# Retention and mixture of experts: the first expert's first 16 products in two halves, and the work around them in another order

## The chip, the cores and the metric

The kernel runs on one core of a Trainium2 chip. A core has five engines with queues of their own: TensorE (PE in the profile; its weight loads are PEld), VectorE (DVE), ScalarE (ACT), GpSimd (POOL) and SyncE (SP), which mostly issues transfers; the transfers themselves run on the core's 16 DMA engines. The metric is the device time of one execution in microseconds, the median of three runs.

## The reference

Retention (a linear attention with decay) over 4 x 8 heads, 768 positions in blocks, and then a layer of 8 experts over its output, where each row goes to the one expert that a gate chooses:

```python
x = attn_out.transpose(0, 2, 1, 3).reshape(B * S, H * D)      # 3072 x 512
logits = x @ w_gate
e_idx = np.argmax(logits, axis=1)
for e in range(E):                                            # 8 experts
    mask = e_idx == e
    h = np.maximum(x[mask] @ w1[e], 0.0)                      # 512 -> 1024
    ye = h @ w2[e]                                            # 1024 -> 512
    out[mask] = gate_w[mask, None] * eom[mask, e, None] * ye
```

`gate_w` is the softmax weight of the chosen expert, `eom` a sigmoid gate.

## The kernel before, in words

**Two stages.** The first computes x in 24 tiles of 128 rows (n = 0 to 23; `NTILE` is 24, `LAST` is 20): transposes, score products, products with v and with the running state. For each group of tiles it works out the gate's logits, the choice of an expert (`route_choose`) and the place of each row in its expert's list (`route_place`), and GpSimd scatters a record of each row into a table in DRAM (`tab_d`, `place_scatter`). The rows themselves are transposed (`stage_d2`, tile `xn`) and stored to `x_d` in DRAM by SP. The second stage takes the experts in order of their number of rows. For each, GpSimd gathers its rows from `x_d` (`gather`, tile `xg`, 32 rows to a transfer), VectorE transposes them (`x_turn`, tile `y`), TensorE multiplies by w1 (`up`, banks `ph`), ScalarE and VectorE take the ReLU apart into two parts (`hhi`, `hlo`), and TensorE multiplies by w2 (banks `py` and `pyr`). Weights come in 32 loads of 1 MB, nearly all by SP (`load_piece`, tile `raw`, three buffers; the second piece is issued by GpSimd) and are split into two parts on ScalarE and VectorE (`whi`, `wlo`).

**The first expert bridges the two.** Which expert has most rows is decided after the first 16 tiles (`RES`). Its first 256 rows are gathered from these, in eight transfers, while the last tiles are still computed: gathers 0 to 3 feed the first transpose `x_turn(0, 0)`, gathers 4 to 7 the second, `x_turn(0, 1)`; both write the same tile `y`. Its other rows, up to 192, are found among tiles 16 to 23 once these have been counted (`mark`, `found`), and gathered as transfers 8 to 13 from `x_d`, after all of x has been stored. So the first expert is worked in two halves: h = 0 (256 columns) and h = 1 (192 columns).

**What sets the order.** It is written out by hand. The list `units` holds the products of half 0 (32 of `up_mm`, each one matmul of 256 columns in fp32, which the trace shows as two instructions; then 16 steps of three products for the w2 side of rows 0 to 255). `fill(k)` issues the next k of them on TensorE, and `settle` the evictions that they have made ready. Between the fills stands the tail of the first stage, on all engines' queues: the places of tiles 20 and 21 (`place`), the choice and places of tiles 22 and 23 (`last`), the marks, two stores of x (`stage_d2(n - 3, 2)` for tiles 20 and 21, called store A here, and `stage_d2(n - 1, 2)` for 22 and 23, store B), two weight loads (`load_piece(2)`, `load_piece(3)`) and the counts. Each engine takes its own instructions strictly in that order. At the end stand the late gathers (`gather(0, 8)`), the sorting of the other experts, the loads of index and tables (which read `tab_d` and so wait for its scatters), and more weight loads.

Of the kernel before, what the change touches and what calls it, by code (L numbers as in the profile page):

```python
# [23 lines left out]
def kernel(  # L24
# [17 lines left out]
    P = 128  # L42
    NPAIR = H // 2
# [6 lines left out]
    NKC = DM // P  # L50
# [884 lines left out]

    hts = {}

    def up_mm(p, fc, h, kc):
        sl = slice((fc % 4) * P, (fc % 4 + 1) * P)
        r = cols(p, h)  # L940
        if kc == 0:
            phs[(p, fc)] = bank(f"ph_{p}_{fc}_{h}")
        if p == 0:
            nb = min(8, NB[p] - 8 * h)
            nc.tensor.matmul(  # L945
                phs[(p, fc)][:, r].rearrange("p (b r) -> p b r", b=nb),
                raws[fc // 4][:, kc, sl],
                ys[(p, h)][:, 0 : nb * P].rearrange("p (b g r) -> p g b r", b=nb, g=NPAIR)[:, kc],
                start=(kc == 0),
                stop=(kc == NKC - 1),  # L950
            )
            return
        whi, wlo = wparts[(p, 0, fc // 4)]
        xhi, xlo = xts[(p, kc)]
        mm3(
            phs[(p, fc)][:, r], (whi[:, kc, sl], wlo[:, kc, sl]), (xhi[:, r], xlo[:, r]),
            kc == 0, kc == NKC - 1,
        )
# [6 lines left out]
    def up_act(p, fc, h):  # L965
        if (p, fc) not in hts:
            hts[(p, fc)] = (slot(f"hhi_{p}_{fc}", F32R), slot(f"hlo_{p}_{fc}", F32R))
        hi, lo = hts[(p, fc)]
        ph = phs.pop((p, fc))
        r = cols(p, h)  # L970
        nc.scalar.activation(out=hi[:, r], in_=ph[:, r], func=AF.Relu)  # L971
        parts = [(r, lo[:, r])]
        if p == 0 and h == 1 and SIDE > 0:
            r0, r1 = slice(r.start, SIDE), slice(SIDE, CAP[0])
            parts = [(r0, lo[:, r0]), (r1, hi[:, CAP[0] : 2 * CAP[0] - SIDE])]
        for r, to in parts:
            nc.vector.scalar_tensor_tensor(  # L977
                out=to, in0=ph[:, r], scalar=0.0, in1=hi[:, r].bitcast(F32),
                op0=ALU.max, op1=ALU.subtract,
            )  # L980
# [192 lines left out]
    held = []  # L1173
    units = []
    acts = []
    for fc in range(NFC):
        for kc in range(NKC):
            act = (lambda fc=fc: up_act(0, fc, 0)) if kc == NKC - 1 else None
            units.append((lambda fc=fc, kc=kc: up_mm(0, fc, 0, kc), act))
    for j in range(2):  # L1180
        for fc in range(NFC):
            act = (lambda j=j: emit_rows(0, j, phs.pop((0, "y", j)))) if fc == NFC - 1 else None
# [13 lines left out]
    with tc.manual_schedule():  # L1196
# [124 lines left out]
        place[0]()  # L1321
        x_turn(0, 0)
        logits(LAST + 2, 2)
        x_turn(0, 1)
        stage_d2(n - 3, 2)
        load_piece(2)
        fill(3)
        for f in place[1:]:
            f()
        place_scatter(len(pending))  # L1330
        logit_rows(LAST + 2)
        fill(6)
        at_once(route_choose(LAST + 2, NTILE))
        for b in range(2):
            mark(LAST, b, 1, late_width)
        last = route_place(LAST + 2, NTILE)
        counts = rank_counts("pcount")
        last[0]()
        fill(6)
        stage_d2(n - 1, 2)  # L1340
        load_piece(3)
        for i in (2, 4, 6):
            last[i]()
        for b in range(2):
            mark(LAST + 2, b, 1, late_width)
        pfound = bank("pfound_late")
        for n in range(RES, NTILE):
            found(pfound, n, (n - RES) // B + 1, late_width, n == RES, n == NTILE - 1)
        settle(2)
        for i in (1, 3, 5, *range(7, len(last))):  # L1350
            last[i]()
        place_scatter(len(pending))
        fill(5)
        row_turn(2, pfound, late_width)
        row_index(0, 2)
        row_join(2, late_width)
        gather(0, 8)
        settle()
# [264 lines left out]
```

## Time and profile before

| | us |
|---|---|
| Median of 3 runs | 412.31 (411.94 to 412.67) |
| The profiled execution | 413.83 |
| its span on the core | 412.2 |
| TensorE busy in it | 397.1 (96%) |
| VectorE, GpSimd, ScalarE busy | 280.3, 233.0, 184.0 |
| DMA, mean rate | 192 GB/s |

Times in the views count from the start of the span. A busy share is an average over the whole kernel, and TensorE's 96% says little about one stage; the stage of this change lies between 114 and 147 us. A group of instructions of the timeline gives the start of the first, the time from there to the end of the last, and how many; ends of matmuls are modelled, so that one matmul's duration is longer than the distance to the next, and steps are read from start to start.

### The profile page before, as it was taken

The numbers are of one execution on the slowest core, as the hardware profiler recorded it, in microseconds if no ns is written. First come the engines' busy times: TensorE is split into PE (matmuls) and PEld (weight loads), VectorE is DVE, ScalarE is ACT, GpSimd is POOL, SyncE is SP. The second block draws the span as 40 slices with busy tenths as digits, with TensorE's granted clock in tenths as the row PEclk, the third lists the DMA queues.
The fourth block names the chain that finished last, engine by engine and source line by source line (L and its number), as shares of the span: only waits on it lengthen the run. The fifth ranks groups of instructions, "written<-read, shape, count | busy, mean of one in ns | idle before, by whom it ended". The sixth has DMA issues, their size and how long they took to land.

```text
span 412.2 us, 10314 instructions
## 1 busy us (share of the span) xinstructions
PE 397.1 (96%) x3767; PEld 364.2 (88%) x3767; DVE 280.3 (68%) x798; ACT 184.0 (45%) x450; POOL 233.0 (57%) x305
## 2 busy tenths in 40 slices
PE   8999989799969999999999999999999999999995
PEld 5879978688858898999999999999999989989985
DVE  3858786678867639778669757957965874863611
ACT  3757656578413325446045325604713542542500
POOL 2567877755876777874583666376386266211002
PEclk9999999999989999999999999999999999999998
DMA  9999999998968844744369648757946985461001
GB/s 179 225 206 254 230 220 233 254 224 198 286 196 249 242 164 105 241 147 139 127 185 308 220 130 237 242 183 188 320 151 172 300 258 167 129 214 64 0 26 48
DMA packets 102116, 78.96 MB, mean 192 GB/s; under 512 B 66348, under 2 KB 78128, under 8 KB 102064
## 3 DMA queue, kind: packets, MB, share of 16 engines
q1 hardware_dynamic: 93264, 63.85, 55.5%
q0 software_dynamic: 6544, 14.15, 11.1%
q10 hardware_dynamic: 2256, 0.30, 0.5%
q8 instruction: 30, 0.49, 0.5%
q14 instruction: 22, 0.18, 0.2%
HBM read 62.45 MB, written 16.21 MB: 191 GB/s over the span
## 4 chain that ended last, share of the span: by engine, by line
PE 75%; DMA 12%; SPq 6%; DVE 3%; issue 1%; POOL 1%; ACTq 0%; POOLq 0%; DVEq 0%
PE ph_None L83 10%; PE ph_None L82 10%; PE ph_None L81 10%; PE py L82 6%; PE py L83 6%; PE py L81 6%; PE pyr L82 4%; PE pyr L81 4%; PE pyr L83 4%; SPq L175 3%; PE ps L389 3%; PE ph L945 3%; SPq L168 3%; DMA tab_d<-rec,idx 3%; PE po L433 2%; DMA xg<-x_d,rows 2%
## 5 line engine op out<-in xcount | busy, mean ns | idle before, releaser
L894 POOL DMA_INDIRECT xg<-x_d,rows x103 | 114.5, 1112 | 63.7 <-issue 34.7
L971 ACT ACTIVATE hhi<-ph_None 128x400 fp32r<-128x400 f32 (+4 forms) x56 | 28.1, 501 | 120.5 <-PE ph_None L83 115.6
L136 DVE TENSOR_TENSOR wlo<-raw,whi 128x512 fp32r<-128x512 f32 x120 | 79.6, 684 | 0.7 <-ACT whi L127 0.5
L83 PE MATMUL ph_None<-xhi,wlo 128*128 128x400 f32 (+4 forms) x224 | 76.3, 341 | 0.0
L81 PE MATMUL ph_None<-xhi,whi 128*128 128x400 f32 (+4 forms) x224 | 76.3, 341 | 0.0
L82 PE MATMUL ph_None<-xlo,whi 128*128 128x400 f32 (+4 forms) x224 | 76.3, 341 | 0.0
L127 ACT CAST whi<-raw 128x512 fp32r<-128x512 f32 x120 | 70.0, 614 | 0.0
L977 DVE SCALAR_TENSOR_TENSOR hlo<-ph_None,hhi 128x400 fp32r<-128x400 f32 (+4 forms) x56 | 31.8, 568 | 37.2 <-ACT hhi L971 37.0
L398 DVE TENSOR_TENSOR at<-ps,decay 128x512 f32<-128x512 f32 x48 | 31.2, 683 | 22.5 <-PE ps L389 22.2
L83 PE MATMUL py<-hhi,wlo 128*128 128x400 f32 (+2 forms) x128 | 44.6, 348 | 0.0
L82 PE MATMUL py<-hlo,whi 128*128 128x400 f32 (+2 forms) x128 | 44.6, 348 | 0.0
L81 PE MATMUL py<-hhi,whi 128*128 128x400 f32 (+2 forms) x128 | 44.6, 348 | 0.0
L81 PEld LDWEIGHTS ph_None<-xhi,whi 128*128 128x128 f32 x224 | 42.1, 188 | 0.4
L82 PEld LDWEIGHTS ph_None<-xlo,whi 128*128 128x128 f32 x224 | 42.1, 188 | 0.4
L83 PEld LDWEIGHTS ph_None<-xhi,wlo 128*128 128x128 f32 x224 | 42.1, 188 | 0.3
L1092 POOL DMA_INDIRECT out_dram<-yn,table x12 | 13.3, 1112 | 49.5 <-DVE yn L1165 31.9
L349 ACT COPY qT<-pq 64x256 f32<-64x256 f32 x88 | 34.7, 394 | 2.5 <-PE pq L341 1.7
L81 PE MATMUL pyr<-whi,hhi 128*128 128x512 f32 (+1 forms) x88 | 34.6, 393 | 0.0
L82 PE MATMUL pyr<-wlo,hhi 128*128 128x512 f32 (+1 forms) x88 | 34.3, 390 | 0.0
L83 PE MATMUL pyr<-whi,hlo 128*128 128x512 f32 (+1 forms) x88 | 34.3, 390 | 0.0
L699 POOL DMA_INDIRECT tab_d<-rec,idx x24 | 24.6, 1024 | 14.9 <-DVE rows L853 4.5
L945 PE MATMUL ph<-y,raw 128*128 128x256 f32 (+1 forms) x128 | 26.9, 369 | 3.4 <-issue 3.2
(211 smaller groups left out, 717.2 us busy)
## 6 DMA issues: line engine op xcount, KB each, us to landing
raw<-in_moe_w_dram SPq DMA_DIRECT2D x31, 1024.0 KB
x_d<-xn SPq DMA_DIRECT2D x12, 512.0 KB
qkv<-in_k_dram SPq DMA_DIRECT2D x38, 128.0 KB
qkv<-in_v_dram SPq DMA_DIRECT2D x19, 256.0 KB
qkv<-in_q_dram SPq DMA_DIRECT2D x36, 128.0 KB
yd<-yo SPq DMA_DIRECT2D x12, 256.0 KB
yr<-yd SPq DMA_DIRECT2D x48, 64.0 KB
xg<-x_d,rows POOLq DMA_INDIRECT x103, 3.4
```

The costliest lines, as they stand in the source:

```text
L81: nc.tensor.matmul(ps, a[0], b[0], start=first, stop=False)
L82: nc.tensor.matmul(ps, a[0], b[1], start=False, stop=False)
L83: nc.tensor.matmul(ps, a[1], b[0], start=False, stop=last)
L127: nc.scalar.copy(out=hi, in_=src)
L136: eng.tensor_tensor(out=lo, in0=src, in1=hi.bitcast(F32), op=ALU.subtract)
L349: copies = [lambda r=r, view=view, src=src: nc.scalar.copy(out=view(qT[r]), in_=src) for r, view, src in query_parts(pq)]
L398: nc.vector.tensor_tensor(out=at, in0=ps.rearrange("p (g t) -> p g t", g=NPAIR), in1=dec[:, j], op=ALU.mult)
L699: nc.gpsimd.indirect_dma_start(out=tab_d, out_offset=bass.IndirectOffsetOnAxis(ap=idx, axis=0), in_=rec, in_offset=None, bounds_check=P * ...
L894: nc.gpsimd.indirect_dma_start(out=xg[(p, b // 4)][:, (b % 4) * P : (b % 4 + 1) * P], out_offset=None, in_=x_q[0 : 4 * rows], in_offset=ba ...
L945: nc.tensor.matmul(phs[(p, fc)][:, r].rearrange("p (b r) -> p b r", b=nb), raws[fc // 4][:, kc, sl], ys[(p, h)][:, 0 : nb * P].rearrange(" ...
L971: nc.scalar.activation(out=hi[:, r], in_=ph[:, r], func=AF.Relu)
L977: nc.vector.scalar_tensor_tensor(out=to, in0=ph[:, r], scalar=0.0, in1=hi[:, r].bitcast(F32), op0=ALU.max, op1=ALU.subtract,)
```

## The change

`up_mm` takes a `part`. For fc 0 to 3 of the first expert the product of 256 columns becomes two of 128: part 0 reads the first 512 columns of `y` (rows of gathers 0 to 3), part 1 the second 512. The list `units` has part 0 of fc 0 to 3 first, then part 1 of them, then fc 4 to 7 as before; the eviction comes after part 1. In the tail, the fills and the steps between them are put in another order.

```diff
-    def up_mm(p, fc, h, kc):
+    def up_mm(p, fc, h, kc, part=None):
...
-        if kc == 0:
+        if kc == 0 and not part:
             phs[(p, fc)] = bank(f"ph_{p}_{fc}_{h}")
         if p == 0:
-            nb = min(8, NB[p] - 8 * h)
+            nb, y0 = min(8, NB[p] - 8 * h), 0
+            if part is not None:
+                nb, y0, r = 4, 4 * P * part, slice(P * part, P * part + P)
...
-                ys[(p, h)][:, 0 : nb * P].rearrange("p (b g r) -> p g b r", b=nb, g=NPAIR)[:, kc],
+                ys[(p, h)][:, y0 : y0 + nb * P].rearrange("p (b g r) -> p g b r", b=nb, g=NPAIR)[:, kc],
...
-    for fc in range(NFC):
-        for kc in range(NKC):
-            act = (lambda fc=fc: up_act(0, fc, 0)) if kc == NKC - 1 else None
-            units.append((lambda fc=fc, kc=kc: up_mm(0, fc, 0, kc), act))
+    for part, fcs in ((0, range(4)), (1, range(4)), (None, range(4, NFC))):
+        for fc in fcs:
+            for kc in range(NKC):
+                act = (lambda fc=fc: up_act(0, fc, 0)) if kc == NKC - 1 and part != 0 else None
+                units.append((lambda fc=fc, kc=kc, part=part: up_mm(0, fc, 0, kc, part), act))
...
         logits(LAST + 2, 2)
+        fill(8)
+        for f in place[1:]:
+            f()
+        for b in range(2):
+            mark(LAST, b, 1, late_width)
+        place_scatter(len(pending))
         x_turn(0, 1)
+        logit_rows(LAST + 2)
+        fill(8)
+        at_once(route_choose(LAST + 2, NTILE))
         stage_d2(n - 3, 2)
         load_piece(2)
-        fill(3)
-        for f in place[1:]:
-            f()
-        place_scatter(len(pending))
-        logit_rows(LAST + 2)
-        fill(6)
-        at_once(route_choose(LAST + 2, NTILE))
-        for b in range(2):
-            mark(LAST, b, 1, late_width)
         last = route_place(LAST + 2, NTILE)
+        fill(4)
         counts = rank_counts("pcount")
         last[0]()
-        fill(6)
+        fill(4)
         stage_d2(n - 1, 2)
         load_piece(3)
         for i in (2, 4, 6):
             last[i]()
         for b in range(2):
             mark(LAST + 2, b, 1, late_width)
+        fill(10)
         pfound = bank("pfound_late")
...
-        settle(2)
         for i in (1, 3, 5, *range(7, len(last))):
             last[i]()
         place_scatter(len(pending))
-        fill(5)
+        settle(1)
+        row_index(0, 2)
+        fill(2)
         row_turn(2, pfound, late_width)
-        row_index(0, 2)
         row_join(2, late_width)
```

On TensorE, right behind the logits of the last two tiles (`pl`; `ph_k` is the bank of fc = k, four matmuls each over kc; `raw` the weights):

```order
-L945 MATMUL ph_0_0_2625<-y_0_2605,raw_2390 128x256 x3
+L947 MATMUL ph_0_0_2618<-y_0_2605,raw_2390 128x128 x4
+L947 MATMUL ph_1_0_2623<-y_0_2605,raw_2390 128x128 x4
 L492 MATMUL pl_2607<-ident,lT_2616 128x128
-L945 MATMUL ph_0_0_2625<-y_0_2605,raw_2390 128x256
-L945 MATMUL ph_1_0_2651<-y_0_2605,raw_2390 128x256 x4
-L945 MATMUL ph_2_0_2656<-y_0_2605,raw_2390 128x256
+L947 MATMUL ph_2_0_2653<-y_0_2605,raw_2390 128x128 x4
+L947 MATMUL ph_3_0_2658<-y_0_2605,raw_2390 128x128 x4
+L947 MATMUL ph_0_0_2618<-y_0_2605,raw_2390 128x128 x4
 L741 LDWEIGHTS ones
```

Sixteen half products of part 0 now stand where before nine whole ones stood, and part 1 of fc 0 comes next; the counts (L741) stay behind them.

On VectorE, from the first transpose of gathered rows (`y` from `xg_0`) on; `xn` from `xT` are the transposes for store A, `pr` the places of tiles 20 and 21:

```order
 L911 STREAM_TRANSPOSE y_0_2605<-xg_0_2153 128x512
-L911 STREAM_TRANSPOSE y_0_2605<-xg_1_2373 128x512
-L516 STREAM_TRANSPOSE xn_2619<-xT_2379 128x512
-L516 STREAM_TRANSPOSE xn_2619<-xT_2468 128x512
 L672 TENSOR_REDUCE pr_2601<-ex_2585 128x2
 L663 TENSOR_TENSOR pr_2601<-pr_2601,ebase 128x16
```

The second transpose and the two for store A leave their place ahead of the places of tiles 20 and 21.

Further on in the same queue of the changed kernel, at the end of the choice for tiles 22 and 23 (`cm`, `oh`) and the places of these (`pr`, `sl`):

```order
+L582 TENSOR_REDUCE cm_2664<-pl_2607 128x2
+L583 TENSOR_TENSOR oh_2638<-pl_2607,cm_2664 128x16
+L516 STREAM_TRANSPOSE xn_2677<-xT_2379 128x512
+L516 STREAM_TRANSPOSE xn_2677<-xT_2468 128x512
+L516 STREAM_TRANSPOSE xn_2703<-xT_2519 128x512
+L516 STREAM_TRANSPOSE xn_2703<-xT_2565 128x512
+L663 TENSOR_TENSOR pr_2695<-pr_2695,ebase 128x16
```

All four transposes for stores A and B now stand in a row behind that choice; before, two marks and store B's two stood there. The second transpose of gathered rows stands ahead of the choice, behind the marks of tiles 20 and 21. The order of the instructions on SP and on GpSimd is the same before and after.

## Rows read from the trace of the kernel before

**Rows 1.** Waits of TensorE from 118.2 us on: total, times, longest (us).

```profile
PE ph L945 <- issue: 3.2, 1, 3.2
PE ph L945 <- DVE y L911: 0.2, 1, 0.2
```

**Rows 2.** Stretches: length, busy PE, PEld, DVE, ACT, POOL; PEclk, DMA share, GB/s.

```profile
114.95:118.17 3.22, 0.00 (x0) 0.03 (x1) 0.81 (x2) 0.27 (x1) 2.33 (x3) 1.00 0.19 44
...
119.50:123.00 3.50, 3.50 (x10) 2.80 (x9) 3.29 (x20) 0.69 (x3) 2.73 (x5) 0.51 1.14 374
...
147.00:200.00 53.00, 53.00 (x276) 49.62 (x275) 38.95 (x114) 24.28 (x57) 36.57 (x40) 1.00 0.52 160
```

**Rows 3.** Chain of waits, in order of time: start, length (us), what.

```profile
114.76 2.58 DMA xg<-x_d,rows
...
123.45 5.64 DMA x_d<-xn
129.09 4.27 DMA tab_d<-rec,idx
...
138.44 7.63 DMA xg<-x_d,rows
...
146.69 3.33 PE ph L945 x19
...
157.33 0.23 PE pyr L81
```

**Rows 4.** VectorE's timeline: start, us, instruction, count, idle before and its releaser.

```profile
114.10 0.71 DVE L911 STREAM_TRANSPOSE y<-xg 128x512 f32<-128x512 f32 x1
117.36 0.71 DVE L911 STREAM_TRANSPOSE y<-xg 128x512 f32<-128x512 f32 x1 [2.55 <-DMA xg<-x_d,rows]
118.00 1.26 DVE L516 STREAM_TRANSPOSE xn<-xT 128x512 f32<-128x512 f32 x2
...
120.47 0.21 DVE L496 TENSOR_REDUCE lg<-pl 128x32 f32<-128x64 f32 x1
...
121.65 0.72 DVE L595 TENSOR_SCALAR marks<-slot_no,lead,sl 128x192 bf16<-128x192 bf16 x2
...
136.57 2.50 DVE L136 TENSOR_TENSOR wlo<-raw,whi 128x512 fp32r<-128x512 f32 x4
```

**Rows 5.** Timeline of SP's queue, 119 to 141 us: transfers as issued.

```profile
119.29 0.37 SPq L523 DMA_DIRECT2D x_d<-xn  x1
...
123.45 0.36 SPq L523 DMA_DIRECT2D x_d<-xn  x1
124.01 0.38 SPq L114 DMA_DIRECT2D raw<-in_moe_w_dram  x1
133.37 0.36 SPq L824 DMA_DIRECT2D index<-tab_d  x1
...
134.54 4.22 SPq L114 DMA_DIRECT2D raw<-in_moe_w_dram  x2
```

**Rows 6.** Timeline of POOL: the first and the last of the six late gathers.

```profile
131.37 1.07 POOL L894 DMA_INDIRECT xg<-x_d,rows  x1 [1.29 <-DVE keys L745]
...
138.44 1.50 POOL L894 DMA_INDIRECT xg<-x_d,rows  x1 [0.30 <-issue]
```

**Rows 7.** Stretches as in rows 2, for the DMA share.

```profile
118.60:121.20 2.60, 2.60 (x11) 2.14 (x10) 2.43 (x17) 0.22 (x1) 2.25 (x3) 0.68 0.99 388
121.20:131.20 10.00, 10.00 (x59) 8.64 (x58) 7.08 (x33) 2.35 (x7) 6.72 (x10) 0.91 1.05 289
132.60:134.80 2.20, 2.20 (x12) 1.92 (x12) 2.16 (x5) 1.36 (x3) 1.75 (x2) 1.00 0.25 48
135.50:144.00 8.50, 8.50 (x39) 7.01 (x38) 5.28 (x13) 2.45 (x5) 6.29 (x6) 1.00 0.97 279
```

**Rows 8.** TensorE's timeline: four transposes of 128 columns, 34 products of 256.

```profile
100.03 0.66 PE L341 MATMUL pk<-ident,k 128*128 128x128 f32 x4
...
128.08 7.53 PE L945 MATMUL ph<-y,raw 128*128 128x256 f32 x34
```

**Rows 9.** Weight loads by form, 85 to 150 us: count, busy, mean ns, idle before.

```profile
L945 PEld LDWEIGHTS ph<-y,raw 128*128 128x128 f32 x85 | 16.4, 205 | 6.0 <-issue 3.5 <-PE pyr L83 0.5
```

## The prediction

> **What bounds the kernel now.** I read four views, in this order. First TensorE's own waits: from 118.2 us to the end there are two, 3.2 us at the first product of the first expert and 0.2 us in front of its second half [rows 1]. Then the stretches: TensorE does nothing from 114.95 to 118.17, runs for the 3.5 us from 119.50 to 123.00 at a mean granted share of 0.51 (the 1.2 GHz level), and from 147 on is busy without a gap (53.00 of 53.00 us) [rows 2]. So whatever moves the start of the second half (the 192 late rows, first product at 146.69) moves the end of the kernel by the same amount, and what only moves work before 146.69 is worth nothing by itself.
>
> Third, the chain of waits, to see who sets 146.69 [rows 3]. It is not TensorE's own work. It runs through the second store of x, issued at 123.45, then through gathers, the last of which is issued at 138.44 and lands 7.63 us later, and the transpose y at 146.10. TensorE comes to that point only 0.2 us earlier [rows 1]. So two chains end there together: TensorE's (gap, half clock, products) and the transfers'. The change shortens the first. The question is what it does to the second.
>
> Fourth, the queues under that chain. SP issues store A (tiles 20, 21) at 119.29, a 1 MB weight load right behind it, store B (tiles 22, 23) at 123.45 and another load right behind that [rows 5]. The DMA share is 0.99 from 118.60 to 121.20 and 1.05 from 121.20 to 131.20 [rows 7]: the engines are full, and what SP issues is served in the order of issue. The first late gather goes at 131.37 [rows 6], since it must read what store B wrote (5.64 us to its release in the chain [rows 3]). Then the share falls to 0.25 (132.60 to 134.80) and is 0.97 again from 135.50 to 144.00 [rows 7], when the next loads, issued in a row from 134.54 on [rows 5], run in front of the last gathers: the same kind of gather that took 2.58 us at 114.76 takes 7.63 us at 138.44 [rows 3].
>
> **The change part by part.** *Halves.* The first 16 products (two instructions each, 128x256) become 32 of 128 columns. An instruction of 256 columns costs 0.216 us at full clock: 34 of them in 7.53 us, of which some 0.4 is the modelled tail of the last one, so 33 steps in 7.13 [rows 8]. One of 128 columns with fresh 128x128 weights: four transposes in 0.66 us, less a tail of some 0.29, so 0.123 a step [rows 8], against 0.108 by columns alone. 64 instructions so cost 6.9 to 7.9 us where 32 cost 6.9. Upper bound, if the weight load (205 ns mean [rows 9]) hid under nothing: 64 x 0.205 = 13.1, +6.2 us. I take 0.123, the row nearest in shape: +1.0 us, on TensorE's chain only.
>
> The Trainium skill speaks against halving: "TensorE: Matmul & The Clock Gate", section "Back-to-back issue gap", says that in a stream of weight loads and matmuls both set the spacing, and gives 81 ns for 128 columns in bf16 where columns alone would need about 54. By that ratio an instruction here would cost 0.162 us and the halves +3.5, an estimate from the page; TensorE would then stand 2.5 us later than I put it below, and the third rival would gain on my forecast. The transposes' 0.123 speaks for the smaller price; no product of this shape stands in the trace.
>
> *The gap.* Part 0 needs only the first transpose y, started at 114.10 and 0.71 us long [rows 4], so products start at 114.95 instead of 118.17: 3.2 us. Without the gap nothing puts the clock down at 119.5; rows at the lower level put that at (1 - 0.51) x 3.50 = 1.7 us [rows 2]. TensorE's chain to the second half gets 3.2 + 1.7 - 1.0 = 3.9 us shorter. That is 146.5 - 3.9 = 142.6. It also meets its weights: the second load behind the stores has landed when the share is down, at 132.6 [rows 7]; then come a first quarter on ScalarE (0.6, like VectorE's), four quarters on VectorE in 2.50 us [rows 4], and nine steps of three products at 0.23 us [rows 3] after the last of them: 132.6 + 0.6 + 2.5 + 6.2 = 141.9, plus what the load itself slips (below). From either side TensorE is at the second half at about 142.6.
>
> *VectorE's order.* The second y waits until 117.36 for its gathers, as before; its follower starts at 118.00 [rows 4]. Before, the two transposes for store A came first, then places, choice and marks, then store B's two. Now places and marks fill the wait before 117.36, and behind the second y come the choice (120.47 to 121.65, 1.18 us [rows 4]) and then four transposes. Store A was issued 1.29 us after its first transpose had started at 118.00 [rows 4, 5]; now that starts at 118.00 + 1.18, so A goes at 120.47, **1.18 us later**. Store B goes two more transposes (1.26 us [rows 4]) after A, near 121.7, **1.8 us earlier**. SP's order is the same: A, load, B, load.
>
> *What the transfers do with that.* B is behind A and a 1 MB load in a full queue, so an earlier issue buys nothing, while A's later issue moves the whole queue. Not all 1.18 us: before, A also stood behind the load that POOL had issued, which filled the engines up to 121.2 (share 0.99 [rows 7]), 1.9 us after A's issue. If a store needs as long as that to start in any case, the slip is 1.18; if it starts as soon as the load of 134.54, of which the share shows traffic from 135.5 on (1.0 us), 120.47 + 1.0 = 121.5 against 121.2, so 0.3. Bounds 0.3 to 1.2; I take 0.8, since A has a full queue ahead of it in the trace and the lone load is the farther row. B's landing, the first gather, the scatters behind the second load, SP's index load at 133.37 (which waits for the last scatter, 4.27 us after 129.09 [rows 3]) and the loads behind it all move by it. Gathers and loads keep their order, so the last gather still lands behind a load: **second half at 146.69 + 0.8 = 147.5**.
>
> *POOL* has the same order; its scatters go at its own pace (the last at 129.09 [rows 3]) and are covered by the wait for B. The counts, the places of the last tiles and the join of the late indices are short steps like those of the choice and are hidden by that same wait; uncovered they would cost 1.18 us for every six of them [rows 4].
>
> *The new gap.* TensorE now waits from 142.6 to 147.5, some 4.9 us, against 0.2 before. The one idle stretch of the trace that long, 3.22 us, was followed by 1.2 GHz for about 3.5 us, costing 1.7 [rows 2]. After this one every product lies on the path to the end. Part of the slow time can fall into the wait itself: 0.9 to 1.7, I take 1.5.
>
> **Sum.** Slip of the transfers +0.8, clock +1.5, gain on TensorE's chain 0 (it ends in a wait): +2.3 us. The profiled execution took 413.83 us (span 412.2, the rest around it unchanged); the median is 412.31, 1.5 lower, and the sum goes on both: 416.1 and **414.6 us**.
>
> **Rivals.** *The transfers let go (faster).* If store B lands by its own issue, 1.8 us earlier, or if the last gather comes in front of the load it now waits behind (issued in the 4.22 us from 134.54 [rows 5]; the gather goes at 138.44, so they are about 1 us apart), the gather lands about 4 us earlier and TensorE's chain decides. The point is about 1 us of shift between gathers and loads. Then the second half starts near 142.9 and nothing is idle: -3.8, 408.5 us. For it: VectorE's 2.50 us of splits, beside which the last gather's issue takes POOL 1.50 us where the first took 1.07 [rows 6], end earlier. Against it: the share of 1.05 around B, and that gathers and loads hang on the same queue. "DMA: Bandwidth & Descriptors", section "Queues, rings and completion order" of the Trainium skill says that each engine takes turns between queues packet by packet, by which a gather would not wait for a whole load; the 7.63 us at 138.44 speak against that here.
>
> *No clock loss.* If the halves cost their upper bound, TensorE comes at 146.5 - 4.9 + 6.2 = 147.8 and doesn't wait; or it waits and the clock stays up. Then the slip remains, +0.8 (or TensorE's own +1.1): 413.1 us.
>
> *The halves do nothing:* the first y would have to be ready as late as the second. Its start at 114.10 [rows 4] excludes that but for a different landing of the gathers; about 412.3 us.
>
> **How the numbers follow.** Slip and clock 0.52 (414.6; own range 412.9 to 416.0: slip 0.3 to 1.2, clock 0.3 to 2.5); transfers let go 0.22 (408.5, some of it only partly, to 412); no clock loss 0.23 (413.1); nothing 0.03. A measurement of this kernel can tell some 0.2%, 0.8 us. The third case lies on that border: 0.13 of it counts as the same, 0.10 as slower. So faster 0.22, same 0.16, slower 0.62. A range from 411.0 to 416.0 leaves out most of the second case and a little above.
>
> **What would show it.** In the changed profile: first product of the first expert at about 115 and no half clock at 119.5 (the gap's term); its 128-column instructions at 0.11 to 0.16 us; store A issued at 120.5 and B at 121.7; first late gather at about 132, not 131.4; TensorE idle for 3 to 5 us just before the first product of the second half, and 0.5 in the clock behind it. I am wrong if that gather goes before 131, if the last one lands within 4 us of its issue, or if TensorE doesn't wait there.

## The result and the profile after

The changed kernel took **419.20 us** in the median of 4 executions (418.52 to 420.46) beside 412.49 for the kernel before (4 executions, 411.94 to 414.14): ratio 1.0124, interval [1.0089, 1.0159], slower. In a later run (after_third, below), with 12 executions beside 35, it took 416.24 against 413.46: ratio 1.0072 [1.0042, 1.0101]. The ratios leave out executions more than 1.5% above the shortest of their kernel, and they are not the quotients of the medians beside them (419.20 by 412.49 would be 1.0163). The forecast was 414.6, range 411.0 to 416.0: the sign came as forecast, both times lie outside the range. The profiled execution of after took 418.52 us, its span 416.7, against 413.83 and 412.2 before.

TensorE's waits from 114.9 us on, in the changed kernel (total, times, longest):

```profile
PE ph L947 <- DVE y L911: 4.5, 1, 4.5
PE pl L481 <- issue: 1.2, 1, 1.2
...
PE pyr L81 <- ACT whi L127: 0.3, 1, 0.3
PE pyr L82 <- DVE wlo L136: 0.2, 1, 0.2
```

The gap of 3.2 us and the wait of 0.2 of [rows 1] have become one wait of 4.5 us in front of the second half. Stretches of after (length, busy PE, PEld, DVE, ACT, POOL; PEclk, DMA share, GB/s):

```profile
119.50:123.00 3.50, 3.50 (x38) 3.49 (x37) 3.33 (x10) 0.78 (x3) 1.60 (x2) 1.00 0.81 312
145.20:149.70 4.50, 0.09 (x1) 0.00 (x0) 0.53 (x2) 0.00 (x0) 3.58 (x4) 0.97 0.99 262
149.76:153.00 3.24, 3.24 (x11) 3.24 (x12) 0.48 (x1) 0.31 (x1) 2.39 (x3) 0.53 0.49 158
153.00:200.00 47.00, 47.00 (x244) 43.81 (x243) 35.54 (x104) 23.97 (x57) 30.07 (x33) 1.00 0.48 142
```

Full clock where [rows 2] has 0.51; then nothing for 4.5 us with the DMA share at 0.99, then 0.53, the 1.2 GHz level, and full from 153 on. TensorE's timeline (start, us, instruction, count, idle before):

```profile
115.10 0.41 PE L481 MATMUL pl<-xT,wgs 128*32 128x128 f32 x5
116.68 0.63 PE L481 MATMUL pl<-xT,wgs 128*32 128x128 f32 x11 [1.17 <-issue]
117.24 2.05 PE L947 MATMUL ph<-y,raw 128*128 128x128 f32 x16
119.13 0.27 PE L492 MATMUL pl<-ident,lT 128*128 128x128 f32 x1
119.24 2.84 PE L947 MATMUL ph<-y,raw 128*128 128x128 f32 x24
```

The halves run behind the first y, and sixteen instructions go by from 117.24 to 119.13, 0.118 us each; 24 take 2.84 us, less the modelled tail of the last (0.27), 0.112 each. VectorE, SP and GpSimd, as in rows 4, 5 and 6:

```profile
118.10 0.71 DVE L911 STREAM_TRANSPOSE y<-xg 128x512 f32<-128x512 f32 x1 [0.27 <-DMA xg<-x_d,rows]
119.44 0.23 DVE L496 TENSOR_REDUCE lg<-pl 128x32 f32<-128x64 f32 x1 [0.63 <-PE pl L492]
...
120.64 2.48 DVE L516 STREAM_TRANSPOSE xn<-xT 128x512 f32<-128x512 f32 x4
```

```profile
121.96 0.37 SPq L523 DMA_DIRECT2D x_d<-xn  x1
122.51 0.38 SPq L114 DMA_DIRECT2D raw<-in_moe_w_dram  x1
123.14 0.73 SPq L523 DMA_DIRECT2D x_d<-xn  x1
...
137.09 4.20 SPq L114 DMA_DIRECT2D raw<-in_moe_w_dram  x2
```

```profile
133.97 1.09 POOL L894 DMA_INDIRECT xg<-x_d,rows  x1 [1.47 <-DVE hlo L979]
...
141.27 1.01 POOL L894 DMA_INDIRECT xg<-x_d,rows  x1 [0.30 <-issue]
```

Store A goes at 121.96 (119.29 in [rows 5]), B 1.18 us behind it, the first late gather at 133.97 (131.37 in [rows 6]), the last at 141.27; the chain of waits of after ends like that of [rows 3], 3.07 us later:

```profile
141.27 7.87 DMA xg<-x_d,rows
149.17 0.46 DVE y L911
149.76 12.15 PE ph L947 x64
```

**The first stage must be taken off.** Its code is the same in all kernels, and yet its length differs between executions. The last products po (line 433) end it; groups of after, then of before, then of after_third (durations in ns, first and last start in us):

```profile
L433 PE MATMUL po<-at,qkv x16: 272/273/324, 113.5 to 114.3; 128*64 128x128 f32 x16
```

```profile
L433 PE MATMUL po<-at,qkv x16: 272/273/323, 112.7 to 113.5; 128*64 128x128 f32 x16
```

```profile
L433 PE MATMUL po<-at,qkv x16: 272/273/323, 110.8 to 111.7; 128*64 128x128 f32 x16
```

So the profiles are compared from the start of the last po on. From there to the end of the span: 298.7 us before, 302.4 after (+3.7), 301.6 in after_third (+2.9, span 413.3). This agrees with the +2.8 of the medians there, though before has no profile of that run. Of the +6.7 of the first run's medians, 0.8 lies in the first stage of the profiled executions, and some 2 more in that the profiled execution of after is its fastest while that of before stands above its median. Three of the four executions of before were on record ahead of the result; beside the fourth, 414.14, which came with it, the median of after is 5.1 us longer.

### The profile page after: what moved, and what is told of

It is laid out like the page before. It is cut to its first block, busy times and chain, and to the rows that moved or that the text cites. A ratio compares the mean times of both kernels' runs of the same rounds, so it can differ in the third digit from the quotient of the medians.

```text
span 416.7 us, 10377 instructions
## 1 busy us (share of the span) xinstructions
PE 398.8 (96%) x3799; PEld 365.7 (88%) x3799; DVE 280.6 (67%) x798; ACT 184.4 (44%) x450; POOL 232.1 (56%) x305
## 3 DMA queue, kind: packets, MB, share of 16 engines
q0 software_dynamic: 6544, 14.15, 11.1%
## 4 chain that ended last, share of the span: by engine, by line
PE 79%; DMA 11%; SPq 4%; DVE 3%; issue 1%; POOL 0%; ACT 0%; ACTq 0%; POOLq 0%; DVEq 0%
PE ph_None L81 10%; PE ph_None L83 10%; PE ph_None L82 10%; PE py L82 6%; PE py L83 6%; PE py L81 6%; PE pyr L82 4%; PE pyr L83 4%; PE pyr L81 4%; DMA qkv<-in_q_dram 4%; PE ph L947 3%; PE ps L389 3%; PE po L433 3%; DMA raw<-in_moe_w_dram 3%; PE po L413 2%; SPq L168 2%
## 5 line engine op out<-in xcount | busy, mean ns | idle before, releaser
L894 POOL DMA_INDIRECT xg<-x_d,rows x103 | 112.6, 1094 | 67.3 <-issue 33.9
L979 DVE SCALAR_TENSOR_TENSOR hlo<-ph_None,hhi 128x400 fp32r<-128x400 f32 (+4 forms) x56 | 31.8, 569 | 37.4 <-ACT hhi L973 37.1
L81 PE MATMUL pyr<-whi,hhi 128*128 128x512 f32 (+1 forms) x88 | 34.8, 395 | 0.3 <-ACT whi L127 0.3
L82 PE MATMUL pyr<-wlo,hhi 128*128 128x512 f32 (+1 forms) x88 | 34.5, 392 | 0.2 <-DVE wlo L136 0.2
L947 PE MATMUL ph<-y,raw 128*128 128x128 f32 (+2 forms) x160 | 27.0, 330 | 4.5 <-DVE y L911 4.5
```

What stands on the lines that cost most here:

```text
L81: nc.tensor.matmul(ps, a[0], b[0], start=first, stop=False)
L82: nc.tensor.matmul(ps, a[0], b[1], start=False, stop=False)
L894: nc.gpsimd.indirect_dma_start(out=xg[(p, b // 4)][:, (b % 4) * P : (b % 4 + 1) * P], out_offset=None, in_=x_q[0 : 4 * rows], in_offset=ba ...
L947: nc.tensor.matmul(phs[(p, fc)][:, r].rearrange("p (b r) -> p b r", b=nb), raws[fc // 4][:, kc, sl], ys[(p, h)][:, y0 : y0 + nb * P].rearr ...
L979: nc.vector.scalar_tensor_tensor(out=to, in0=ph[:, r], scalar=0.0, in1=hi[:, r].bitcast(F32), op0=ALU.max, op1=ALU.subtract,)
```

## The experiments

All kernels beside before on the same chip. The table gives, from the timelines, the start of the last po, and counted from it: the issue of store A, the last scatter, the first late gather (g) and its distance from A, the transpose y of the last late rows, the second half, and the end of the span.

| kernel | last po | A | last scatter | g | g − A | y | second half | end |
|---|---|---|---|---|---|---|---|---|
| before | 113.5 | 5.8 | 15.6 | 17.8 | 12.1 | 32.6 | 33.2 | 298.7 |
| after | 114.3 | 7.6 | 16.8 | 19.6 | 12.0 | 34.8 | 35.4 | 302.4 |
| after_third | 111.7 | 7.0 | 15.3 | 19.4 | 12.4 | 34.2 | 34.8 | 301.6 |
| e1 halves alone | 115.2 | 6.7 | 15.7 | 18.7 | 12.0 | 33.5 | 34.1 | 301.3 |
| e2 order alone | 112.5 | 7.7 | 16.0 | 19.8 | 12.1 | 34.2 | 34.8 | 300.2 |
| e3 A early | 115.4 | 7.3 | 16.6 | 18.9 | 11.6 | 33.8 | 34.4 | 302.7 |
| e4 kept awake | 113.2 | 7.3 | 13.9 | 19.5 | 12.2 | 33.2 | 34.5 | 299.9 |
| e9 both stores first | 112.3 | 3.0 | 17.3 | 18.6 | 15.7 | 34.0 | 34.6 | 302.7 |
| e10 before, loads behind | 114.1 | 6.0 | 15.8 | 17.1 | 11.1 | 30.2 | 33.1 | 298.5 |
| e11 rows first | 113.4 | 7.7 | 17.0 | 19.7 | 12.0 | 34.4 | 35.0 | 302.8 |
| e14 later loads | 112.5 | 7.4 | 16.2 | 19.5 | 12.2 | 33.2 | 33.8 | 302.6 |
| e15 all three | 113.3 | 4.0 | 17.4 | 18.7 | 14.7 | 32.0 | 32.6 | 300.5 |

The profiles of e1, e3 and e9 each caught the longest execution of their kernel (418.07, 419.87, 416.91 us); their rows serve for the order within the stretch, and not for the kernel's time.

**The two halves of the change apart.** e1 has the halves with the order of before (against which the diff stands; `units` as in the change):

```diff
+        fill(8)
         x_turn(0, 1)
         stage_d2(n - 3, 2)
         load_piece(2)
-        fill(3)
...
-        fill(6)
+        fill(8)
...
-        fill(6)
+        fill(12)
...
-        fill(5)
+        fill(8)
```

> The halves with the order of before: store A right behind the second transpose y, then places, choice, marks, counts as they stood. Theory 1 (the loss is that store A is issued late, which moves store B's landing, the late gathers and the second half; half clock behind the new wait comes on top): A issued near 119.5, second half near 147, TensorE waits 3 to 5 us in front of it, clock 0.5 behind it, +1.5 us against before: 414.0 us. Theory 2 (the loss lies in the fuller stretch itself: more instructions, the stall inside the logits at 115.5, GpSimd starting later): 417 to 419 us as in the changed kernel, with the second half at 149 although A goes early.

Measured: 412.81 against 414.40, ratio 0.9973 [0.9945, 1.0000]. Neither theory's time: the halves alone cost nothing that shows and may gain a little. A went 1.9 us behind the second y, as before. In its profile, one of its long executions, TensorE waits 1.9 us in front of the second half and is at 0.54 behind it; what its short ones do there isn't shown.

e2 is the new order with whole products (diff against the changed kernel, like those that follow):

```diff
-    for part, fcs in ((0, range(4)), (1, range(4)), (None, range(4, NFC))):
+    for part, fcs in ((None, range(NFC)),):
...
-        fill(8)
...
-        fill(4)
+        fill(2)
...
-        fill(4)
+        fill(2)
...
-        fill(10)
+        fill(6)
```

> Whole products of 256 columns with the new order of the tail (the same products ahead of the same steps, but all behind the second transpose y). Theory 1: TensorE's gap of 3 us and the half clock behind it are back, store A goes at about 120.5, the transfers set the second half at 148 to 149 and TensorE, which comes at about 147, waits too little to lose its clock: 414 to 415.5 us. Theory 2: no more instructions than before, so as before: 412.5 us.

415.69 against 414.40, ratio 1.0054 [1.0013, 1.0095], nearer to theory 1. TensorE's gap and its half clock are there again, and yet it waits 1.1 us in front of the second half, without losing its clock behind it (stretches 147.33 to 150.60 and 117.92 to 122.00; columns as above):

```profile
PE ph L947 <- issue: 3.2, 1, 3.2
PE ph L947 <- DVE y L911: 1.1, 1, 1.1
```

```profile
147.33:150.60 3.27, 3.27 (x20) 3.27 (x21) 0.94 (x4) 0.66 (x2) 2.36 (x4) 1.00 0.68 235
117.92:122.00 4.08, 4.08 (x11) 3.32 (x12) 3.29 (x10) 0.78 (x3) 3.24 (x4) 0.58 0.84 318
```

So the order alone loses time: A 2.0 us later, second half 1.7 us later, with no half product in the kernel. In the medians that is 1.3 us, about half of the 2.8 of the whole change. The other half would be the clock behind the longer wait (e4, below), as far as two chips compare.

e3 puts back one thing in the changed kernel:

```diff
         x_turn(0, 1)
+        stage_d2(n - 3, 2)
+        load_piece(2)
         logit_rows(LAST + 2)
         fill(8)
         at_once(route_choose(LAST + 2, NTILE))
-        stage_d2(n - 3, 2)
-        load_piece(2)
```

> The changed kernel with one thing put back: the two transposes and the issue of store A, and the weight load behind it, stand right behind the second transpose y, ahead of the choice. Theory 1: A at about 120, 2 us earlier than in the changed kernel, second half 1.5 to 2 us earlier; the wait of TensorE shrinks to about 2.5 to 3 us and the clock still falls: 417 to 417.5 us. Theory 2: A earlier, nothing else moves: 419 us.

415.39 against 414.40, ratio 0.9996 [0.9958, 1.0034]. The medians of all ten and 31 executions are 1.0 us apart. So most of the loss is gone, by the ratio all of it, more than expected, as far as numbers of two chips compare: the changed kernel itself did not run on this one. In its profile the second y came 1.65 us later than in after (5.42 against 3.77 behind the last po) and A 1.92 behind it, against 3.86 in after.

e4 keeps TensorE at work in its wait:

```diff
         fill(len(units))
         settle()
+        awake = bank("awake")
+        for _ in range(18):
+            nc.tensor.matmul(awake, blank[:, 0:P], blank, start=True, stop=True)
```

> The changed kernel with 18 matmuls of 512 columns in bf16 (zeros into a bank nobody reads), some 3.9 us at full clock, in TensorE's queue in front of the second half. If the half clock behind the wait costs what its row shows, the second half starts at the same time (149.8) but at full clock, and the kernel ends 1.5 us earlier: 417.7 us. If the clock's loss is elsewhere, or the extra matmuls outlast the wait, 419.2 us or more.

415.45 against 414.40, ratio 1.0021 [0.9984, 1.0057]. The extra matmuls (17 records) ran from 143.88 and ended with the wait; TensorE was then at full clock:

```profile
143.88 4.06 PE L1390 MATMUL awake<-blank 128*128 128x512 bf16 x17
147.77 0.98 PE L947 MATMUL ph<-y,raw 128*128 128x192 f32 x5
```

```profile
147.77:151.00 3.23, 3.23 (x21) 3.22 (x20) 0.48 (x3) 0.66 (x2) 2.50 (x3) 1.00 0.54 173
```

From the second half to the end it took 265.3 us, as before (265.5), where after took 266.9 and after_third 266.8: in these two profiles the half clock costs 1.3 to 1.4 us. The matmuls outlasted the rows by some 0.8 us, so not all of it was gained.

**Which queue it is.** After_third is the changed kernel itself:

> The changed kernel unchanged, beside the next three, on their chip. If its stretch behind the first stage is what makes the loss: 302 to 303 us from the last po to the end (298.7 in before's profile), store A 7.6 us behind that po, first late gather 12 us behind A; the median then stands 3.7 us above that of before, plus or minus what the first stage varies by.

Ratio 1.0072 [1.0042, 1.0101], 2.8 us; the distances came as expected (A 7.0, g 12.4 behind it). Its wait in front of the second half is 4.3 us. Its waits show no stall inside the logits, and A is 0.6 us earlier than in the first profile.

e10 is the kernel before with `load_piece(2)` moved behind store B, in front of `load_piece(3)`.

> The kernel before (whole products, its own order) with SP's order A, B, load, load. If two chains end at the second half there, TensorE's only 0.2 us ahead of the transfers', then making the transfers earlier gains next to nothing by itself: within 0.5 us of before, the wait in front of the second half gone, the 3 us gap and the half clock at 119 still there. If the transfers alone set it: 1 to 3 us faster than before.

413.71 against 413.46, ratio 0.9995 [0.9966, 1.0025]. The first late gather now follows the last scatter at once, the late rows come 2.3 us earlier, and TensorE's only wait from 114.9 us on is the gap:

```profile
129.91 0.99 POOL L699 DMA_INDIRECT tab_d<-rec,idx  x1 [0.30 <-issue]
131.20 1.08 POOL L894 DMA_INDIRECT xg<-x_d,rows  x1 [0.30 <-PE ph L945]
```

```profile
PE ph L945 <- issue: 3.0, 1, 3.0
```

The second half stays at 33.1. That is the reading of the two chains, shown from the other side: earlier transfers alone are worth nothing either.

e11 puts `logit_rows(LAST + 2)` right behind the logits, ahead of the first `fill(8)`.

> The changed kernel with one transpose of the logits (TensorE L492) and its sum on VectorE put right behind the logits, ahead of the first eight half products, as store A waited for the choice and the choice for that transpose: the choice then starts right behind the second y, A goes some 0.7 us earlier (at 6.9 behind the last po instead of 7.6), and the second half by as much: 0.7 us faster than the changed kernel. If A's place behind the choice is all that counts: the same time.

417.18 against 413.46, ratio 1.0053 [1.0017, 1.0088]; no gain that can be told from the changed kernel. In its profile the second y came 1.1 us later, and A at 7.7: between y and A lay 2.8 us instead of 3.9 (3.1 in after_third). Inconclusive as a time.

e9 puts `stage_d2(n - 3, 2)` right behind `x_turn(0, 0)`, into VectorE's wait, and both loads behind store B.

> The changed kernel with store A in VectorE's wait for the second y, and SP's order A, B, load, load. Counted from the last po: A at 3, B at 7.5 to 8.5, the scatters set the first late gather at 17.9 to 18.3, the late rows are there at 28 to 31. Then TensorE's own chain sets the second half, at 31 (33.2 in before, 35.4 in the changed kernel), and no half clock follows: 2 us faster than before, 6 us faster than the changed kernel. If the halves' gain on TensorE was never real, or the later loads hold the products with w2: as before or slower.

412.50 against 413.46, ratio 0.9956 [0.9921, 0.9991], 3.7 us under the changed kernel on that chip. The means of all twelve and 35 executions are only 0.4 us apart. Half of its executions lie between 409.7 and 411.6, half between 413.4 and 416.9; the profile is of the longest. There the scatters set the first gather, as expected (17.3 and 18.6), but they were late themselves, and the late rows came at 34.0.

**Runs on chips with stalls.** On two chips every kernel took some 20 to 25 us more; TensorE stood in many places with nothing released. The changed kernel's waits there, from 126 us on (of the first, the 3.0 us end where the late rows have come, in front of the second half; the other 4.5 in five places are such stalls):

```profile
PE ph L947 <- issue: 7.5, 6, 3.0
PE pcount L741 <- DVE oh L583: 1.6, 1, 1.6
PE pl L492 <- issue: 0.9, 1, 0.9
```

Before itself ran from 426 to 441 us there, so ratios to it say little, and these kernels are read against each other.

> The changed kernel once more, beside the runs that follow, since the first stage, which the change doesn't touch, was 0.8 us longer in its profile than in that of before (start of its last product po 114.33 against 113.53), and by up to 1.9 us in other profiles. If the loss of 6.7 us is all the change's own, the difference to before is 6 to 7 us here too. If the first stage's length varies from run to run and only the stretch behind it is the change's, what the profiles show of that stretch is left: 302.4 us from the last po to the end against 298.7, so 3.7 us.

441.88 against 436.93, ratio 1.0307 [1.0225, 1.0389].

e6 moves store A and `load_piece(2)` right behind `x_turn(0, 0)`; e7 only puts the two loads behind store B.

> The changed kernel with store A (its two transposes, its issue, the load behind it) moved ahead into VectorE's wait for the second y: A at about 3 us behind the last po instead of 7.6. Theory 1 (the first late gather goes 12 us after A's issue, as in all six profiles so far, until the scatters on GpSimd set it): now the scatters set it, at 17.9 to 18.3 instead of 19.6, the second half starts 1.5 to 2.5 us earlier, and what is left of TensorE's wait costs less clock: 2 to 4 us faster than the changed kernel, about as before. Theory 2 (A's issue doesn't matter, GpSimd's late scatters or the fuller stretch do): as the changed kernel.

> The changed kernel with SP's order A, B, load, load instead of A, load, B, load; A and B are issued as late as there. Theory 1, in its form that store B's landing sets the late gathers and that it waits behind the load: B lands some 4 us earlier, the scatters set the first gather at 18.1 instead of 19.6, second half 1 to 2 us earlier, if the loads, which now land later (the first by 2 us), don't hold TensorE's products with w2: 1 to 3 us faster than the changed kernel. If the queue's order doesn't matter (the gathers wait for something else): the same.

437.56 (ratio 1.0191 [1.0108, 1.0275]) and 437.24 (1.0196 [1.0125, 1.0266]): 4.3 and 4.6 us under the changed kernel's 441.88, against 2 to 4 and 1 to 3 expected. From the last po: A at 3.0 and first gather at 17.9 in e6, A at 10.1 and first gather at 16.6 in e7, against 10.6 and 21.8 in after_again. Second half at 33.4 and 31.8 against 36.0. In e7 VectorE no longer waits for the late rows; both transposes stand behind a step that waited for TensorE:

```profile
152.17 0.75 DVE L1167 TENSOR_SCALAR yn<-pyr,table 128x512 f32<-128x512 f32 x1 [0.24 <-PE pyr L83]
152.84 1.04 DVE L911 STREAM_TRANSPOSE y<-xg 128x512 f32<-128x512 f32 x2
```

e8 is e6 with `place_scatter(len(pending))` for the last tiles behind `gather(0, 8)`.

> As the kernel with store A in the wait, and the last two scatters (records of tiles 22 and 23) behind the late gathers on GpSimd instead of ahead of them. The index load of the next expert, which waits for the scatters, and the two weight loads behind it then go some 5 us later, behind the late gathers. Theory 1 with its second part (the last gathers land late because those weight loads run in front of them): first late gather at 14 to 16 behind the last po, last one landed 3 to 4 us after its issue instead of 7.9, the second half set by TensorE's own chain at 30 to 31 (35.4 in the changed kernel), no half clock: 5 to 6 us faster than the changed kernel, 1 to 3 us faster than before, unless the next expert's rows come too late. If the transfers were not what holds the second half: no gain.

442.02, ratio 1.0299 [1.0217, 1.0380]: no gain. The miss has a cause of its own. The next expert's index, now late, stands in front of the late rows' transposes in VectorE's queue:

```profile
158.97 0.17 DVE L848 SCALAR_TENSOR_TENSOR rowf<-index 32x16 f32<-32x16 int32 x1 [6.62 <-DMA index<-tab_d]
...
160.57 1.03 DVE L911 STREAM_TRANSPOSE y<-xg 128x512 f32<-128x512 f32 x2
```

**The loads in front of the last gathers.** e12 lets GpSimd issue the next two loads behind the late gathers; e13 is that with both stores first. e14 and e15 are the same two on a chip without stalls.

```diff
...
-        load_piece(4)
+        load_piece(4, nc.gpsimd)
         expert_regs(2, order_i[:, 2:E], E - 2)
-        load_piece(5)
         for j in range(4):
             split_quarter(2, j)
             fill(3)
             settle()
+        load_piece(5, nc.gpsimd)
```

> The changed kernel with the next two weight loads (those SP issues from 137 us on, in front of the last late gathers) issued by GpSimd behind these gathers. Store A, the first late gather (12 us behind A) and the gathers' issues stay as they are: 19.5 and 27 behind the last po. If the last gathers' 7 to 8 us to landing are these loads, they now land in 3 to 4 us, the late rows are there at 30 to 31 instead of 34.5, TensorE's own chain sets the second half at about 31 and no half clock follows: 3 to 5 us faster than the changed kernel, 1 to 2 us faster than before. Then half of the forecast's error is that it took the loads' place in front of the gathers as fixed to the gathers. If the landing is slow for another reason (the gathers' own packets, the outputs of the stretch): the same as the changed kernel, or slower, as GpSimd has two more issues.

> Both stores first (A in the wait for the second y, B, then load, load) and the next two loads behind the late gathers on GpSimd. Late rows at 26 to 29 behind the last po, second half by TensorE's own chain at 30.5 to 31.5, no half clock, whatever way the scatters fall: 2 to 2.5 us faster than before (ratio 0.994 to 0.995). If TensorE's chain is itself held (weights behind both stores, the next expert's rows behind the loads on GpSimd): as before.

With stalls: 440.52 and 438.27 against 436.30 (ratios 1.0225 [1.0084, 1.0366] and 1.0181 [1.0038, 1.0323]); last gather to y 4.2 us in e12, 6.4 in after_again. So the loads in front are part of that time; the changed kernel did not run beside e12, and what this is worth can't be told from it.

> The same edit as in the kernel with the next two loads behind the late gathers; its first run fell on a chip on which every kernel takes some 24 us longer, TensorE standing in many places with nothing released (issue), so that the size of the effect can't be read there. On a chip like that of before's profile: the last gather lands in 4 us instead of 7.9, late rows at 30 to 31.5 behind the last po, TensorE's wait under 1 us, 3 to 4 us faster than the changed kernel, 0.5 to 1 us faster than before. If the loads are not it: as the changed kernel (2.8 us slower than before).

> The same edit as in the kernel with both stores first and the next two loads behind the late gathers, on such a chip: late rows at 28 to 30, second half set by TensorE's own chain at 30.5 to 31.5 (33.2 in before), no half clock: 2 us faster than before (ratio 0.995). If TensorE's chain is held elsewhere, as before.

Without: 415.85 and 415.57 against 413.93, ratios 1.0035 [1.0010, 1.0060] and 1.0062 [1.0035, 1.0088]; both misses. In e14 SP's next load took the free place, beside the last gather (issued at 139.48), and y came 6.25 us behind it, not 4:

```profile
139.34 0.37 SPq L114 DMA_DIRECT2D raw<-in_moe_w_dram  x1
```

```profile
145.73 0.45 DVE L911 STREAM_TRANSPOSE y<-xg 128x256 f32<-128x256 f32 x1 [5.39 <-DMA xg<-x_d,rows]
```

e15 brought the second half to 32.6, 0.6 ahead of before, although TensorE had waited 2.4 us for weights on the way there. Behind it, it waited 1.3 us for the next expert's rows, and from the second half to the end it took 267.9 us instead of 265.5; where the other 1.1 us went isn't shown (TensorE's waits):

```profile
PE ph L947 <- DMA raw<-in_moe_w_dram: 2.4, 2, 1.7
PE ph_None L81 <- ACT xhi L925: 1.0, 1, 1.0
...
PE ph_None L82 <- DVE xlo L929: 0.3, 1, 0.3
```

Last, e9 once more (e16), and e9 with 12 of e4's matmuls (e17), again on a chip with stalls:

> The kernel with both stores first once more: its median was 0.44% under that of before, but its profile caught one of its long executions (416.91 of 409.68 to 416.91), with the late rows at 34.0 behind the last po. If the gain is the stretch's, a profile of a usual execution shows the late rows at 29 to 31 and the second half at 31 to 32 (33.2 in before), and the ratio is 0.994 to 0.997 again. If the late rows come at 34 here too, the gain is not where I look for it.

> The same with 12 matmuls of 512 columns in bf16 in front of the second half (2.6 us), as in the kernel kept awake. Where the late rows come late (34), they save the half clock, 1 to 1.5 us; where they come early (31), they cost up to 2 us. Over its executions: within 0.5 us of the kernel with both stores first, with a smaller spread; a profile with the late rows at 33 or later shows full clock behind the wait.

433.95 and 435.27 against 432.95, ratios 1.0076 [1.0031, 1.0120] and 1.0084 [1.0038, 1.0130]. The late rows came early (27.3 and 26.7), the second half at 30.8, and at 32.9 where the matmuls outlasted the wait. That e9 is faster than before rests on one chip and on the ratio there; it isn't settled.

## Why the prediction was right or wrong

**The reading of the bound held.** The second half is where two chains end; e10 shows that the transfers' alone gains nothing, e1 that TensorE's alone gains next to nothing. *The gap and the clock at 119.5* went as forecast, the first product 2.3 us later than that (117.24 for 114.95), of which 0.8 is the first stage and 1.2 the stall inside the logits; in after_third it comes 1.6 us behind the last po, where 1.4 was forecast. *The halves* cost 0.112 to 0.118 us an instruction, less than the 0.123 taken. The Trainium skill's "TensorE: Matmul & The Clock Gate", section "Back-to-back issue gap", led to an estimate of 0.162; the row disagrees for fp32 of 128 columns, and the measurement decides.

**TensorE's arrival.** Forecast 142.6 in before's profile, 29.1 behind the last po; measured 31.0 (149.76 less the wait of 4.47). Most of the difference is the stall of 1.17 us inside the logits and 0.5 us for the splits of the load behind store B. Nothing came of it, since the wait hid it.

**Store A.** Forecast: 1.18 us later by the choice, B 1.2 behind A. After_third shows this to a tenth: A +1.2, B 1.19 behind A. In the first profile 0.6 us more: the stall in the logits made the transpose L492 late (VectorE's 0.63 us in front of `lg`), and A stands behind the choice that needs it. The forecast costed the order on VectorE, but not that the choice's input now waits on TensorE behind eight half products.

**The step that failed: the transfers' slip.** I took 0.8 of A's 1.18 us, since A had a full queue ahead of it. But the first late gather goes 12.0 to 12.4 us behind A's issue in before, after, after_third, e1, e2, e4, e11 and e14, wherever A, load, B, load stand in that order (11.6 in e3). What that gather waits for is store B: by its completions in the trace B has landed 16.9 us behind the last po in before, 18.7 in after and 18.5 in after_third, and the gather goes 0.9 us later each time. B lands late although it is issued 1.1 and 1.7 us earlier than in before, since the load ahead of it, which SP issues right behind A, has moved with A. B's own issue to its landing takes 7.0 us in before and 9.9 in after; without that load ahead it takes 3.3 in e10 and 4.0 in e9.

The queue ahead of A gave nothing back that lasted. A smaller distance shows only where GpSimd's load had been issued 12.8 us ahead of A instead of 2.9 to 5.7: in after_again and e12, on chips with stalls, the gather goes 11.1 to 11.2 us behind A. With SP's loads behind B, the last scatter stands right in front of the gather instead (1.3 us in e7, e9, e10, e15, e16 and e17, 2.6 in e13).

The late rows then moved by 1.6 us in after_third and by 2.3 in after. So the term was 1.6 to 2.3, not 0.8: A's delay (1.2 and 1.9) passed on whole, and 0.4 us more. In after_third these lie between A's issue and the gather (12.4 for 12.1), in after between the first late gather and the last y (15.2 for 14.8); why is open. The upper bound of 1.2 held only A's delay as forecast.

**The clock** was forecast at 1.5 and is 1.3 to 1.4 by both profiles of the changed kernel; e4 takes it away. But this price isn't fixed. Behind waits of 3.6, 4.3 and 4.1 us in the profiles of e3, e9 and e11, TensorE was at the lower level for about twice as long, and from the second half to the end it took 268.3, 268.1 and 267.8 us, 2.3 to 2.8 more than before. The stretch from e3's second half on:

```profile
149.80:156.00 6.20, 6.20 (x21) 6.20 (x22) 1.25 (x5) 0.66 (x2) 4.98 (x6) 0.53 0.41 129
```

Which of the two prices the other executions of the changed kernel paid isn't shown.

**The sum.** +1.6 and +1.3 make +2.9, and the medians of the run with after_third say +2.8, against a forecast of +2.3. The first run's +6.7 holds 3.7 from the stretch; the rest is in what the range left out. The first median stands 4.6 us above the forecast: the stretch accounts for 1.4 of that (3.7 for 2.3), and the larger part lies outside it. I moved the sum from one profiled execution to a median as if the first stage were constant; it spans 111.7 to 115.4 us in the profiles without stalls. And the median I moved it to, 412.31, was a low one: before's medians in the later runs without stalls are 413.5 to 414.4. That the first run's other executions differed in the first stage is argued, not shown: they have no profile, and the cause of that part stays open.

**The rivals.** *Transfers let go* did not come by itself: the last gather landed 7.87 us behind its issue. The 1 us that I put between that gather and the load ahead of it was misread: the two issues from 134.54 take 4.22 us in all, the second so starts near 138.4, less than 0.1 us ahead of the gather. What the Trainium skill's "DMA: Bandwidth & Descriptors", section "Queues, rings and completion order", says of engines that take turns between queues would let a gather pass a load; neither after nor e14 (6.25 us) shows that. *No clock loss* is what e2 shows, where TensorE waits only 1.1 us, but there the halves are missing.

## What to carry to other kernels

Where two chains end at one place, shortening the one is worth nothing unless the other gets slack first; what looked like an idle gap was the cover of the other chain. An issue in an engine's order (here store A on VectorE's path to SP, and with it the load that SP issues next) was a term of the slow chain with its full size, plus what its new predecessor waits for: put it in front of such steps, into a wait. And a profiled execution carries stages that the change doesn't touch; compare from their end on, and put their spread into the range.

## What the runs showed that I had not expected

- In the first profile of after TensorE stood 1.17 us in the middle of one run of 16 equal matmuls, with nothing released ("issue"). The profile's instruction queue moved 16 KB shortly before (from 114.28 to 115.23). The Trainium skill's "Runtime: NRT & Kernel Launch", section "Instruction fetch mechanics", says that such a refill is mostly hidden; before's lay in the gap of 3.2 us. The profiles of e1, e4 and e14 have such a stall in the logits too (1.2, 0.8 and 0.9 us), that of after_third has none. That the refill is the cause is argued only; no run separates it.
- In the median the kernel before takes 412 to 414 us on some chips and 433 to 437 on others, the changed one 416 to 419 and 442. On the chips with the longer times such stalls stand throughout (4.5 us in five places in the view above).
- In front of the second half a wait of 1.1 us left the clock at full (e2). One of 1.9 us was followed by 0.54 in e1 and by full clock in e8 (the line below), waits of 4.3 to 4.5 us (both profiles of after) by 0.53 to 0.54. Filling the wait kept the clock up (e4).

```profile
161.74:165.00 3.26, 3.26 (x20) 3.26 (x21) 0.93 (x4) 0.66 (x2) 2.38 (x3) 1.00 0.87 256
```
